# Sigmoid attention and a two-layer network on one core: the products of attention are moved to float32 in the four quarters of the TensorE array

## The chip, the core and the metric

The kernel runs on one core of one Trainium2 chip. The metric is the device time of one launch in microseconds (us); lower is better. "Granted clock" is the share of TensorE's full speed (2.4 GHz) that the profile reports.

## The reference

```python
q, k, v: [8, 12, 448, 64]                      # batch, heads, positions, head size
scores = np.matmul(q, k.transpose(0, 1, 3, 2)) / 8 - np.log(448)
attn = 1.0 / (1.0 + np.exp(-scores))           # a sigmoid, no sum over a row
x = np.matmul(attn, v)                         # -> [8 * 448, 768], heads side by side
h = x @ w_in                                   # [768, 2048]
g = np.maximum(0.01 * h, h)
out = g @ w_out                                # [2048, 768]
```

All inputs and the output are float32.

## The kernel before

The work has three stages, one after the other on TensorE. **Attention** writes x in blocks of [128 columns, 448 positions]. **Stage f** multiplies x by w_in, **stage a** multiplies g by w_out. Stages f and a use sums and differences of blocks (a fast matrix product, so fewer products), and each float32 operand is split there into a high and a low part of type float32r, a type that takes one pass on the array where float32 takes two instructions; a product is then high x high + high x low + low x high. The sums of blocks and the low parts are made on VectorE (DVE), the high parts and copies on ScalarE (ACT).

Attention goes over 48 pairs of heads (`Pair`), two pairs in a *round*, 24 rounds of five *slots*. Program order is kept on every engine: `slot` first emits what is due in the slot by rank (`at`, `later`), then its products; `prepare(room)` then lets VectorE do up to `room` us of other work, which decodes w_in and w_out and builds the sums of their blocks (tiles `wr`, `wd`, `ws`) and the sums of blocks of x (`x_s`). All matrix operations, copies and DMAs are recorded on one helper line, L159, so the trace is read by tile names:

- `qk`: queries and keys of a pair, [2 x 64 rows, 2, 448]: one head in rows 0 to 63, the other in rows 64 to 127. `qks`: their high and low parts.
- `sc_<pair>_<chunk>`: scores in PSUM, [128 keys, 2 heads, 448 queries], for chunks 0 to 2 of 128 keys. A chunk takes 2 heads x 3 products of [64 rows x 128 columns] in float32r: the two heads stand in the upper and lower half of the array.
- `s_<pair>_<chunk>`: the sigmoid of it in SBUF, by ACT, one instruction a chunk.
- The last 64 keys of two pairs are handled together as chunk 3 (`last_scores`): four float32 products of 64 x 64, one in each quarter of the array.
- `pv_<pair>`: the sums with v in PSUM, for both pairs of a round in two banks. A chunk of a pair is two float32 products of [128 rows x 64 columns], one head in each half of the columns (`attn_v`); `last_v` adds chunk 3 with four products in the quarters.
- `x_...`: `Block.keep` copies the two banks to SBUF on ACT, and sums and stores of x follow.

PSUM is used as four buffers of two banks each, for `sc` and `pv` alike. The scores and sums of a round read:

```python
mm(out=ps[:, j, cols], lhsT=self.parts[me, kp, 1, c * P:c * P + P], rhs=self.parts[me, qp, 0, cols], ...)
mm(self.pv[me, :S], lhsT=self.v[:, (NK - 1) * j + c, :], rhs=self.a[c][:, j], start=c == 0, ...)
works = [lambda: whole(x), lambda: whole(y), x.attn_v, y.attn_v, lambda: ending(y, more[0] if more else None)]
```

A float32 product appears in the trace as two instructions of TensorE, a float32r product as one.

Of the kernel before, what the change touches and what calls it, by code (L numbers as in the profile page):

```python
# [12 lines left out]
F32R = mybir.dt.float32r  # L13
# [5 lines left out]
P = 128  # L19


ROOM = 1.7, 2.2, 2.1, 0.7, 0.2
SLOT, READ, STEP, LATE = 2.4, 1.09, 0.7, 1.1
CAST, SOON, HOLD = 3, 2, 4
PAUSE = 1
IDLE = 7


TILES, MORE, LAST, JOIN = 13, 3, 6, 6
RESULTS = 8  # L30
ROTS = 3
EARLY, FIRST, SOON2, JOINT = 12, 9, (2, 5), 26
# [89 lines left out]
def attn_ffn_kernel(ctx: ExitStack, tc: tile.TileContext, qk, v, w_in, w_out, out):  # L122
# [13 lines left out]
    S = qk.shape[3]  # L136
    NP = qk.shape[0] // B
    D = P // 2
    NK = 4
# [9 lines left out]
    heads = [slice(j * D, j * D + D) for j in range(2)]  # L149
# [7 lines left out]
    def pinned(issue):  # L157

        return lambda *args, **kw: tc.keep_in_program_order(issue(*args, **kw))  # L159
# [12 lines left out]
    mm, dma = pinned(nc.tensor.matmul), pinned(nc.sync.dma_start)  # L172
    copy, act, dma_act = (pinned(x) for x in (nc.scalar.copy, nc.scalar.activation, nc.scalar.dma_start))
    vcopy = pinned(nc.vector.tensor_copy)
# [3 lines left out]
    def sub(to, x, y):  # L178
        vec(out=to, in0=x, in1=y, op=ALU.subtract)

    def add(to, x, y):
        vec(out=to, in0=x, in1=y, op=ALU.add)
# [10 lines left out]
    def at(when, rank, *fns):  # L193

        chores.setdefault(when, []).extend((rank, fn) for fn in fns)

    def later(slots, *fns, first=False):
        at(now + slots, 0 if first else 5, *fns)

    def slot(work=None, behind=()):  # L200
        nonlocal now
        todo = sorted(chores.pop(now, ()), key=lambda x: x[0])
        for rank, fn in todo:
            if rank not in behind:
                fn()
        if work is not None:
            work()
        for rank, fn in todo:
            if rank in behind:
                fn()  # L210
        now += 1
# [5 lines left out]
    class Wide:  # L217
# [18 lines left out]
        def high(self):  # L236
            copy(out=self.t[:, 0], in_=self.t[:, 1].bitcast(F32))

        def low(self):
            sub(self.t[:, 1], self.t[:, 1].bitcast(F32), self.t[:, 0])  # L240
# [43 lines left out]
    ps = ExitStack()  # L284
# [37 lines left out]
    def drop(t, slots=1):  # L322
# [3 lines left out]
    attn = ExitStack()  # L326
    vs = attn.enter_context(tc.tile_pool(name="vs", bufs=4, reuse_waits="tile"))
    shift(attn, "pad1", 64)
    raws, spl, ats, made1, wr3 = (attn.enter_context(tc.tile_pool(name=name, bufs=bufs, reuse_waits="tile")) for name, bufs in (
        ("raws", 4), ("spl", 2), ("at", 6), ("sums", 1), ("wr3", 1)))  # L330
    warm = shift(ctx, "warm", 32, "right")
    tiles(ctx, "r", "right", TILES)
    shift(ctx, "pad2", 64, "right")
# [161 lines left out]
    xs, sums = {}, []  # L495

    HALVES = slice(0, S // 2), slice(S // 2, S)
    KEYS = slice(0, 2 * P), slice(2 * P, S)

    SPLIT = slice(0, 2 * S - D)  # L500

    def flat(x):
        return x.rearrange("p a s -> p (a s)")[:, SPLIT]

    class Pair:


# [21 lines left out]
            self.room = t[:, 2 * NK * D:2 * NK * D + 2 * S].rearrange("p (a b) -> p a b", a=2)  # L529
            dma(out=self.v[:, :n], in_=v[self.i, :, :n])  # L530

        def high(self, how=None):
            self.parts = spl.tile([P, 2, 2, S], F32R, tag="qks", name=f"qks_{self.i}")
            (how or copy)(out=flat(self.parts[:, 0]), in_=flat(self.raw))

        def low(self):
            sub(flat(self.parts[:, 1]), flat(self.raw), flat(self.parts[:, 0]))

        def split(self):

            self.parts = spl.tile([P, 2, 2, S], F32R, tag="qks", name=f"qks_{self.i}")
            high, low = self.parts[:, 0], self.parts[:, 1]
            for cols in HALVES:
                copy(out=high[:, 0, cols], in_=self.raw[:, 0, cols])
            for n, cols in enumerate((KEYS[0], slice(2 * P, S - D))):
                vcopy(out=high[:, 1, cols], in_=self.raw[:, 1, cols])
                sub(low[:, 1, cols], self.raw[:, 1, cols], high[:, 1, cols])
                if n == 0:
                    for x in HALVES:
                        sub(low[:, 0, x], self.raw[:, 0, x], high[:, 0, x])  # L550

        def scores(self, h):
            todo, acts = [], []
            for c in range(2 * h, min(2 * h + 2, NK - 1)):
                ps = psum("s", f"sc_{self.i}_{c}")

                for cols in HALVES if self.i == h == 0 else (slice(0, S),):
                    for m, (kp, qp) in enumerate(((0, 0), (0, 1), (1, 0))):
                        for j, me in enumerate(heads):
                            todo.append((c, (m > 0 and c + 1, m, cols.start), dict(  # L560
                                out=ps[:, j, cols], lhsT=self.parts[me, kp, 1, c * P:c * P + P],
                                rhs=self.parts[me, qp, 0, cols], start=m == 0 and cols.start == 0,
                                stop=m == 2 and cols.stop == S, skip_group_check=True)))
                acts.append((c, ps))
            if self.i == h == 0:
                todo.sort(key=lambda x: x[1])
            for n, (c, ps) in enumerate(acts):
                for x in todo if self.i == h == 0 and n == 0 else [x for x in todo if x[0] == c and (self.i or h)]:
                    mm(**x[2])
                self.a.append(self.attn(c, ps))  # L570

        def attn(self, c, ps, s=None):
            if s is None:
# [9 lines left out]
                    mm(ps[rows, j, :S], lhsT=y.raw[me, 1, S - D:], rhs=y.raw[me, 0], start=True, stop=True, skip_group_check=True)  # L583
            self.last = self.attn(NK - 1, ps, pairs[self.i + 1].room)

        def attn_v(self):
            mate = pairs[self.i - 1]
            if self.part == 1:
                self.both = psum("s", f"pv_{self.i}")
            self.pv = (self if self.part == 1 else mate).both[:, self.part - 1]  # L590
            for c in range(NK - 1):
                for j, me in enumerate(heads):
                    mm(self.pv[me, :S], lhsT=self.v[:, (NK - 1) * j + c, :], rhs=self.a[c][:, j], start=c == 0, stop=False,
                       skip_group_check=True)

        def last_v(self):

            x = pairs[self.i - 1]
            for j, me in enumerate(heads):
                for y, rows in ((x, heads[0]), (self, heads[1])):  # L600
                    mm(y.pv[me, :S], lhsT=self.v[rows, 2 * NK - 2 + j, :], rhs=x.last[rows, j],
                       start=False, stop=True, skip_group_check=True)
            block = Block(self.i // 2)
            later(1, lambda: block.keep(x.both), first=True)
            at(now + 2, 8, block.start)

    class Block:
# [7 lines left out]
        def keep(self, pv):  # L615
            xs[self.name] = grab(f"x_{self.p}_{self.name}", F32)
            copy(out=xs[self.name], in_=pv[:, :, :S])

        def store(self, n, t, *gone):

# [56 lines left out]
    pairs = [Pair(i) for i in range(B * NP)]  # L677
# [6 lines left out]
    pairs[1].load_qk()  # L684
    pairs[0].load_v()
    act(out=warm, in_=warm, func=AF.Sigmoid)
    pairs[0].split()
    pairs[2].load_qk()
    pairs[1].load_v()
    next(preps)  # L690
    pairs[1].high(vcopy)
    pairs[1].low()
    pairs[3].load_qk()
    psum = banks("ps_a", dict(s=(4, 2)))

    def whole(x):
        x.scores(0)
        x.scores(1)

    def ending(x, y):  # L700

        if y is not None:
            y.last_scores()
        x.last_v()

    unread = psum("s", "unread")[:, 0]
    for _ in range(IDLE):
        mm(unread[heads[0], :S // 4], lhsT=zeros[:, :D], rhs=zeros, start=True, stop=True)
    slot(lambda: pairs[0].scores(0))
    slot(lambda: pairs[0].scores(1))  # L710
    slot(pairs[0].last_scores)
    rounds = (last + 1) // 2
    items1 = [(p, i, jj) for p in range(NQ) for i in range(len(PRODUCTS1)) for jj in range(2)]
# [6 lines left out]
    for p in range(NQ):  # L720
        for i, n in enumerate(XS):
            if n in XS[:i]:
                continue
            x, t = Own(p, n), when(p, i)
# [5 lines left out]

    for r in range(rounds):
        x, y, *more = pairs[2 * r:2 * r + 6]
        works = [lambda: whole(x), lambda: whole(y), x.attn_v, y.attn_v, lambda: ending(y, more[0] if more else None)]
        if r == 0:

            works = [works[2], works[1], lambda: None, *works[3:]]
        if more:
            z, w = more[:2]
            later(0, z.load_v)
            later(1, w.load_v)  # L740
            later(2, z.high)
            later(3, z.low, w.high)
            later(4, w.low)
        for n, far in enumerate(more[2:]):
            later(1 + 3 * n, far.load_qk)
        for n, work in enumerate(works):
            slot(work)
            prepare(ROOM[n] * (r > 0))

# [17 lines left out]
    psum = banks("ps_f", {f"acc{n}": (1, 2) for n in range(4)})  # L767
# [6 lines left out]
    for g in range(SPLIT1, len(GROUPS1)):  # L774
        for j in range(KQ):
            x = w1[g, j] = Wide(g, j, wb, "wb")
            prepared_by(base + (g - SPLIT1) * 8 + j, x, 0)
    ws = {}
    for p in range(NQ):
        for n, load in STREAM.items():  # L780
            x = ws[p, n] = Streamed(p, n)
# [171 lines left out]
    for q in range(2):  # L953
        for h in range(2):
# [7 lines left out]
            live, last, first = {}, {}, {}  # L962
# [10 lines left out]
            for name, (how, a, b) in sums2[q].items():  # L973
                s = put[q, h, name]
                v = live[name, events[name][0][2]]
                a, b = live[a, name], live[b, name]
# [7 lines left out]
            for i, x in enumerate(PRODUCTS2):  # L984
                k = 2 * NH * q + 2 * i + h
                v = live[x[0], k]
                me = operands[k] = Operand(k, v)
# [194 lines left out]
```

## Time and profile before

| what | value |
|---|---|
| median of 3 runs | 1013.63 us (1013.28 to 1013.64) |
| the profiled execution | 1013.27 us, of which the span from first to last instruction is 1011.5 us |
| attention, until stage f begins | 249.4 us |
| stage f | 384.4 us |
| stage a and the end | 377.7 us |
| TensorE busy | 1006.9 us |

The profile lists busy time by engine, groups of instructions by tile names with the mean duration of one, the idle time before them and what ended it, and the chain of work that ended last. Matmuls are pipelined: a group's mean duration is longer than the distance from one to the next, so distances are read from starts.

### The profile page before, as it was taken

To read this page: it belongs to the slowest core of one execution; us is meant where nothing else is said; L and a number is where in the kernel's file an instruction comes from. 1 tells how busy PE (TensorE), PEld (TensorE's weight loads), DVE (VectorE), ACT (ScalarE), POOL (GpSimd) and SP (SyncE) were. 2 spreads that over 40 slices of the span, in tenths; PEclk is the share of its full clock that TensorE was granted. 3 is DMA by queue.
4 is the path that set the end of the run, shared out by engine and by line. 5 is a ranking of instruction groups with operands and counts; after the bars stand their busy time and mean duration, and the time that the engine had idled before them with its cause. 6 is when DMAs were issued, how large, how long until landed. Compare 5 with 4: busy or idle time off the path is not lost.

```text
span 1011.5 us, 15201 instructions
## 1 busy us (share of the span) xinstructions
PE 1006.9 (100%) x5642; PEld 844.5 (83%) x5642; DVE 853.2 (84%) x1116; ACT 586.2 (58%) x710; POOL 0.3 (0%) x5
## 2 busy tenths in 40 slices
PE   9999999999999999999999999999999999999998
PEld 5555455555999999999999999999999999999998
DVE  5888888887898779888867778799998999999886
ACT  7888888887644454445453655575453456635431
POOL 0000000000000000000000000000000000000000
PEclk9999999999999999999999999999999999999999
DMA  9799899998988997799789979967738698775643
GB/s 326 269 337 370 298 379 324 361 336 276 382 302 241 348 321 266 246 384 311 246 268 315 322 238 362 409 222 255 269 118 321 250 361 326 241 279 164 215 171 109
DMA packets 142025, 291.79 MB, mean 288 GB/s; under 512 B 11136, under 2 KB 71680, under 8 KB 141952
## 3 DMA queue, kind: packets, MB, share of 16 engines
q1 hardware_dynamic: 141088, 290.02, 81.9%
q8 instruction: 44, 0.72, 0.3%
q10 hardware_dynamic: 864, 0.80, 0.2%
q14 instruction: 29, 0.24, 0.1%
HBM read 189.33 MB, written 101.45 MB: 287 GB/s over the span
## 4 chain that ended last, share of the span: by engine, by line
PE 99%; DMA 0%; DVE 0%; ACT 0%; DVEq 0%; issue 0%
PE f L159 38%; PE a L159 36%; PE pv L159 13%; PE sc L159 11%; PE e_z L159 0%; DMA qk<-in_qk 0%; PE e_a L159 0%; DVE o L159 0%; ACT qks L159 0%; DVEq L1178 0%
## 5 line engine op out<-in xcount | busy, mean ns | idle before, releaser
L159 PE MATMUL a<-gh,w 128*128 128x448 f32 x1224 | 342.9, 361 | 0.0
L159 PE MATMUL f<-xh,w 128*128 128x448 f32 x960 | 270.9, 361 | 0.0
L159 PEld LDWEIGHTS a<-gh,w 128*128 128x128 f32 x1224 | 229.3, 187 | 16.9
L159 PE MATMUL a<-gl,w 128*128 128x448 f32 x540 | 196.0, 363 | 0.0
L159 PEld LDWEIGHTS f<-xh,w 128*128 128x128 f32 x960 | 179.9, 187 | 14.3 <-issue 0.7
L159 PE MATMUL f<-xl,w 128*128 128x448 f32 x480 | 174.2, 363 | 0.0
L159 ACT CAST gh<-g 128x896 fp32r<-128x896 f32 x80 | 75.4, 942 | 123.3 <-DVE g L159 108.7
L159 DVE TENSOR_TENSOR h<-h,f 128x896 f32<-128x896 f32 x88 | 95.5, 1085 | 50.4 <-PE f L159 50.2
L159 ACT ACTIVATE s<-sc 128x896 f32<-128x896 f32 x144 | 119.8, 956 | 3.1 <-PE sc L159 3.1
L159 PE MATMUL pv<-s,v 128*64 128x448 f32 x576 | 113.8, 543 | 0.0
L159 ACT COPY h<-f 128x896 f32<-128x896 f32 x56 | 50.1, 910 | 96.5 <-PE f L159 75.2
L159 PEld LDWEIGHTS a<-gl,w 128*128 128x128 f32 x540 | 101.3, 188 | 5.4
L159 DVE TENSOR_TENSOR w<-w 128x768 fp32r<-128x768 f32 x112 | 104.5, 953 | 1.0 <-ACT w L159 1.0
L159 PEld LDWEIGHTS sc<-qks 64*128 64x128 f32 x876 | 79.9, 186 | 23.2 <-issue 16.9
L159 ACT CAST w<-w 128x768 fp32r<-128x768 f32 x112 | 93.1, 832 | 4.0 <-DMA w<-t 4.0
L159 PE MATMUL sc<-qks 64*128 64x448 f32 (+1 forms) x876 | 94.8, 367 | 0.2 <-ACT qks L159 0.2
L159 PEld LDWEIGHTS f<-xl,w 128*128 128x128 f32 x480 | 90.1, 188 | 4.6
L159 PEld LDWEIGHTS pv<-s,v 128*64 128x64 f32 x576 | 39.1, 137 | 63.2 <-issue 54.3
L159 PE MATMUL f<-xh,ws 128*128 128x448 f32 x320 | 91.5, 361 | 0.0
L159 DVE TENSOR_TENSOR gl<-g,gh 128x896 fp32r<-128x896 f32 x72 | 78.3, 1088 | 5.0 <-ACT gh L159 4.5
L159 ACT CAST xh<-xl 128x896 fp32r<-128x896 f32 x64 | 60.3, 944 | 35.5 <-DMA xl<-xd 22.2
L159 DVE TENSOR_TENSOR qks<-qk,qks 128x832 fp32r<-128x832 f32 (+3 forms) x51 | 49.2, 972 | 37.1 <-ACT qks L159 33.9
(79 smaller groups left out, 1072.8 us busy)
## 6 DMA issues: line engine op xcount, KB each, us to landing
w<-t SPq DMA_DIRECT2D x112, 384.0 KB, 4.7
g<-g SPq DMA_DIRECT2D x81, 448.0 KB, 5.8
xl<-xd SPq DMA_DIRECT2D x64, 448.0 KB, 6.4
g<-h SPq DMA_DIRECT2D x64, 448.0 KB, 6.0
qk<-in_qk SPq DMA_DIRECT2D x46, 448.0 KB, 5.6
xd<-x_s SPq DMA_DIRECT2D x36, 448.0 KB, 6.8
xd<-x SPq DMA_DIRECT2D x28, 448.0 KB, 6.6
wr<-in_w_in SPq DMA_DIRECT2D x24, 512.0 KB, 6.6
```

The source lines that it names most:

```text
L159: return lambda *args, **kw: tc.keep_in_program_order(issue(*args, **kw))
```

## The change

- Queries and keys are no longer split: `high`, `low` and `split` go, with the ACT casts and the VectorE subtractions that made `qks`, and its pool. The pool of `qk` has six buffers where it had four.
- A chunk of scores is four float32 products of [64 rows x 64 columns], one in each quarter: head j in rows, each half of the chunk's 128 keys in columns.
- The sums with v take both pairs at once. A chunk's 128 keys are two halves of 64 rows, so a product is [64 rows x 64 columns] and there are two accumulators, `pv_<pair>_0` and `pv_<pair>_1`: into the first goes the upper half of the first pair and the lower half of the second, into the second the other two halves. Chunk 3 goes into the first.
- `Block.keep` copies the second accumulator with ACT a slot earlier than before; a new `Block.add` adds the first one on VectorE, where the copy was before. PSUM still has four buffers of two banks.
- The first slots: all chunks of pair 0 in one slot, no wait for a split. One warm-up product fewer (`IDLE` 6). The shares of `prepare` (`ROOM`) are spread evenly with the same total, 6.9. One tile of x more for the whole run and one fewer later (`TILES`, `MORE`).

```diff
-ROOM = 1.7, 2.2, 2.1, 0.7, 0.2
+ROOM = 1.4, 1.4, 1.4, 1.4, 1.3
...
-TILES, MORE, LAST, JOIN = 13, 3, 6, 6
+TILES, MORE, LAST, JOIN = 14, 2, 6, 6
...
+        def scores(self, c):
+            ps = psum("s", f"sc_{self.i}_{c}")
+            for j, me in enumerate(heads):
+                for n, rows in enumerate(heads):
+                    keys = slice(c * P + n * D, c * P + n * D + D)
+                    mm(ps[rows, j, :S], lhsT=self.raw[me, 1, keys], rhs=self.raw[me, 0], start=True, stop=True,
+                       skip_group_check=True)
+            self.a.append(self.attn(c, ps))
...
+        def attn_v(self, c):
+
+            x = pairs[self.i - 1]
+            if c == 0:
+                self.both = []
+            for n in range(2):
+                if c == 0:
+                    self.both.append(psum("s", f"pv_{x.i}_{n}"))
                 for j, me in enumerate(heads):
-                    mm(self.pv[me, :S], lhsT=self.v[:, (NK - 1) * j + c, :], rhs=self.a[c][:, j], start=c == 0, stop=False,
-                       skip_group_check=True)
+                    for m, (y, rows) in enumerate(((x, heads[n]), (self, heads[1 - n]))):
+                        mm(self.both[n][me, m, :S], lhsT=y.v[rows, (NK - 1) * j + c, :], rhs=y.a[c][rows, j],
+                           start=c == 0, stop=n == 1 and c == NK - 2, skip_group_check=True)
+            if c == NK - 2:
+                self.block = Block(self.i // 2)
+                later(1, lambda: self.block.keep(self.both[1]), first=True)
...
-            block = Block(self.i // 2)
-            later(1, lambda: block.keep(x.both), first=True)
+            block = self.block
+            later(1, lambda: block.add(self.both[0]), first=True)
             at(now + 2, 8, block.start)
...
+        def add(self, pv):
+            add(xs[self.name], xs[self.name], pv[:, :, :S])
...
+        works = [
+            several((x.scores, 0), (y.scores, 0), (x.scores, 1)), several((y.scores, 1), (x.scores, 2), (y.scores, 2)),
+            several((y.attn_v, 0)), several((y.attn_v, 1), (y.attn_v, 2)), lambda: ending(y, more[0] if more else None)]
...
-            later(2, z.high)
-            later(3, z.low, w.high)
-            later(4, w.low)
```

TensorE, the scores of one whole round and the sums with v that follow, before; each `x6` is one chunk, and the output's 128 rows are all columns of the array:

```order
L159 MATMUL sc_4_0_495<-qks_4_451 128x448 x6
L159 MATMUL sc_4_1_496<-qks_4_451 128x448 x6
L159 MATMUL sc_4_2_513<-qks_4_451 128x448 x6
L159 MATMUL sc_5_0_528<-qks_5_464 128x448 x6
L159 MATMUL sc_5_1_529<-qks_5_464 128x448 x6
L159 MATMUL sc_5_2_546<-qks_5_464 128x448 x6
L159 MATMUL pv_4_563<-s_4_0_503,v_4_381 64x448 x2
L159 MATMUL pv_4_563<-s_4_1_511,v_4_381 64x448 x2
L159 MATMUL pv_4_563<-s_4_2_520,v_4_381 64x448 x2
L159 MATMUL pv_4_563<-s_5_0_536,v_5_415 64x448 x2
L159 MATMUL pv_4_563<-s_5_1_544,v_5_415 64x448 x2
L159 MATMUL pv_4_563<-s_5_2_553,v_5_415 64x448 x2
```

The same place in a round of the changed kernel, to the end of the first chunk's sums:

```order
L159 MATMUL sc_6_0_571<-qk_6_378 64x448 x4
L159 MATMUL sc_7_0_578<-qk_7_437 64x448 x4
L159 MATMUL sc_6_1_585<-qk_6_378 64x448 x4
L159 MATMUL sc_7_1_604<-qk_7_437 64x448 x4
L159 MATMUL sc_6_2_611<-qk_6_378 64x448 x4
L159 MATMUL sc_7_2_618<-qk_7_437 64x448 x4
L159 MATMUL pv_6_0_627<-s_6_0_576,v_6_455 64x448
L159 MATMUL pv_6_0_627<-s_7_0_583,v_7_482 64x448
L159 MATMUL pv_6_0_627<-s_6_0_576,v_6_455 64x448
L159 MATMUL pv_6_0_627<-s_7_0_583,v_7_482 64x448
L159 MATMUL pv_6_1_632<-s_6_0_576,v_6_455 64x448
L159 MATMUL pv_6_1_632<-s_7_0_583,v_7_482 64x448
```

The chunks of the two pairs alternate now, each is four products of 64 x 64 in place of six, and a chunk's sums are eight products of 64 x 64, four for each accumulator, where a pair's chunk took two of 128 rows.

VectorE near the end of a round before; `qks` rows are the low parts of the next round's queries and keys, the others are work of `prepare`:

```order
L159 TENSOR_TENSOR ws0_0_557<-wd0_0_410,ws0_0_557 128x2x128
L159 TENSOR_TENSOR qks_6_561<-qk_6_417,qks_6_561 128x832
L159 TENSOR_TENSOR ws0_0_557<-ws0_0_557,wd0_0_410 128x2x128
L159 TENSOR_SCALAR wd0_1_591<-wr0_1_0_466 128x512
L159 TENSOR_TENSOR qks_7_577<-qk_7_476,qks_7_577 128x832
L159 TENSOR_SCALAR wd0_1_591<-wd0_1_591 128x512 x2
L159 SCALAR_TENSOR_TENSOR wd0_1_591<-wr0_1_0_466,wd0_1_591 128x512
L159 TENSOR_TENSOR x_0_s8_677<-x_0_10_379,x_0_20_607 128x896
```

The same place in the changed kernel:

```order
L159 TENSOR_TENSOR ws0_0_519<-ws0_0_519,wd0_0_372 128x2x128
L159 TENSOR_SCALAR wd0_1_566<-wr0_1_0_439 128x512
L159 TENSOR_TENSOR x_0_20_544<-x_0_20_544,pv_4_0_509 128x896
L159 TENSOR_SCALAR wd0_1_566<-wd0_1_566 128x512 x2
L159 SCALAR_TENSOR_TENSOR wd0_1_566<-wr0_1_0_439,wd0_1_566 128x512
L159 TENSOR_TENSOR x_0_s8_625<-x_0_10_334,x_0_20_544 128x896
L159 TENSOR_TENSOR x_0_s13_637<-x_0_s5_507,x_0_20_544 128x896
L159 SCALAR_TENSOR_TENSOR wd0_1_566<-wr0_1_0_439,wd0_1_566 128x512
```

The two `qks` rows are gone, and the row `x_0_20_544<-x_0_20_544,pv_4_0_509` has come in: it reads the first accumulator, so it waits for the last product of its round, and all of `prepare` that follows on VectorE waits behind it.

## Rows read from the trace of the kernel before

**Rows 1.** The page: span; busy us of each engine (share, instructions).

```profile
span 1011.5 us, 15201 instructions
PE 1006.9 (100%) x5642; PEld 844.5 (83%) x5642; DVE 853.2 (84%) x1116; ACT 586.2 (58%) x710; POOL 0.3 (0%) x5
```

**Rows 2.** Windows by stage: busy by engine (instructions), clock, DMA share, GB/s.

```profile
0.00:16.30 16.30, 15.05 (x112) 8.77 (x112) 5.55 (x12) 10.38 (x14) 0.31 (x5) 1.00 0.89 325
16.30:249.40 233.10, 233.10 (x1741) 125.04 (x1741) 196.43 (x340) 197.02 (x262) 0.00 (x0) 1.00 0.93 328
249.40:633.80 384.40, 384.40 (x1921) 360.09 (x1922) 309.25 (x430) 195.94 (x221) 0.00 (x0) 1.00 0.89 304
```

**Rows 3.** The chain that ended last, in order of time: start, us, what.

```profile
3.70 0.39 ACT qks L159
4.08 0.04 issue
4.13 3.64 PE sc L159 x33
...
16.29 3.84 PE sc L159 x36
...
26.46 3.84 PE sc L159 x36
30.30 4.66 PE pv L159 x24
34.96 0.91 PE sc L159 x8
35.88 0.75 PE pv L159 x8
36.63 3.84 PE sc L159 x36
...
249.38 384.39 PE f L159 x1920
```

**Rows 4.** Timeline of the weight loads (PEld) inside one round.

```profile
25.16 0.15 PEld L159 LDWEIGHTS pv<-v 64*64 64x64 f32 x4 [0.22 <-issue]
25.53 0.15 PEld L159 LDWEIGHTS pv<-v 64*64 64x64 f32 x4 [0.22 <-issue]
...
30.66 0.14 PEld L159 LDWEIGHTS pv<-s,v 128*64 128x64 f32 x2 [0.23 <-issue]
...
34.04 0.14 PEld L159 LDWEIGHTS pv<-s,v 128*64 128x64 f32 x2 [0.23 <-issue]
```

**Rows 5.** Timeline, all engines, of the same round and its end.

```profile
27.38 4.99 ACT L159 ACTIVATE s<-sc 128x896 f32<-128x896 f32 x6
...
35.70 0.93 PE L159 MATMUL pv<-v 64*64 64x448 f32 x8
...
35.94 0.92 ACT L159 ACTIVATE v<-sc 128x896 f32<-128x896 f32 x1 [2.04 <-PE sc L159]
```

**Rows 6.** Groups of DVE and ACT, 16.3 to 249.3: busy, mean ns, idle.

```profile
L159 DVE TENSOR_TENSOR qks<-qk,qks 128x832 fp32r<-128x832 f32 x45 | 45.9, 1023 | 30.5 <-ACT qks L159 27.4 <-DMA xd<-x_s 1.7 <-DMA ts<-ws 1.3
...
L159 ACT CAST qks<-qk 128x832 fp32r<-128x832 f32 x44 | 38.1, 953 | 0.0
L159 ACT COPY x<-pv 128x896 f32<-128x896 f32 x23 | 20.8, 904 | 0.0
```

**Rows 7.** The page's groups: VectorE adding from PSUM.

```profile
L159 DVE TENSOR_TENSOR h<-h,f 128x896 f32<-128x896 f32 x88 | 95.5, 1085 | 50.4 <-PE f L159 50.2
```

**Rows 8.** Timeline of the first microseconds, ACT's queue and TensorE's warm-up.

```profile
0.73 1.38 ACTq L159 DMA_DIRECT2D qk<-in_qk  x3
1.03 2.88 PE L159 MATMUL unread<-zeros 128*64 128x112 f32 x14 [1.03 <-DVE zeros L682]
5.98 0.33 SPq L159 DMA_DIRECT2D qk<-in_qk  x1
```

**Rows 9.** DMA issues at 1.1:1.6 and 5.9:6.3: KB each, us to landing.

```profile
qk<-in_qk ACTq DMA_DIRECT2D x2, 112.0 KB, 3.0
...
qk<-in_qk SPq DMA_DIRECT2D x1, 448.0 KB, 7.7
```

**Rows 10.** Waits from 249 to 256: who waited for whom, us, times, longest.

```profile
ACT x L159 <- DMA xd<-x_s: 3.4, 1, 3.4
...
PEld f L159 <- ACT x L159: 0.3, 1, 0.3
```

More of the change, by code (lines that the diff above doesn't have):

```diff
@@ L25 @@
 PAUSE = 1
-IDLE = 7
-TILES, MORE, LAST, JOIN = 13, 3, 6, 6
+IDLE = 6
+TILES, MORE, LAST, JOIN = 14, 2, 6, 6
 RESULTS = 8
@@ L328, in attn_ffn_kernel @@
     shift(attn, "pad1", 64)
-    raws, spl, ats, made1, wr3 = (attn.enter_context(tc.tile_pool(name=name, bufs=bufs, reuse_waits="tile")) for name, bufs in (
-        ("raws", 4), ("spl", 2), ("at", 6), ("sums", 1), ("wr3", 1)))
+    raws, ats, made1, wr3 = (attn.enter_context(tc.tile_pool(name=name, bufs=bufs, reuse_waits="tile")) for name, bufs in (
+        ("raws", 6), ("at", 6), ("sums", 1), ("wr3", 1)))
     warm = shift(ctx, "warm", 32, "right")
@@ L498, in attn_ffn_kernel @@
     KEYS = slice(0, 2 * P), slice(2 * P, S)
-    SPLIT = slice(0, 2 * S - D)
-    def flat(x):
-        return x.rearrange("p a s -> p (a s)")[:, SPLIT]
     class Pair:
@@ L530, in load_v @@
             dma(out=self.v[:, :n], in_=v[self.i, :, :n])
[L532 to L570, printed above, removed]
+        def scores(self, c):
[6 more added lines that the diff above has]
+            self.a.append(self.attn(c, ps))
@@ L584, in last_scores @@
             self.last = self.attn(NK - 1, ps, pairs[self.i + 1].room)
[L586 to L591, printed above, removed]
-                for j, me in enumerate(heads):
-                    mm(self.pv[me, :S], lhsT=self.v[:, (NK - 1) * j + c, :], rhs=self.a[c][:, j], start=c == 0, stop=False,
-                       skip_group_check=True)
+        def attn_v(self, c):
[5 more added lines that the diff above has]
+                    self.both.append(psum("s", f"pv_{x.i}_{n}"))
+                for j, me in enumerate(heads):
+                    for m, (y, rows) in enumerate(((x, heads[n]), (self, heads[1 - n]))):
[4 more added lines that the diff above has]
+                later(1, lambda: self.block.keep(self.both[1]), first=True)
         def last_v(self):
@@ L599, in last_v @@
             for j, me in enumerate(heads):
-                for y, rows in ((x, heads[0]), (self, heads[1])):
-                    mm(y.pv[me, :S], lhsT=self.v[rows, 2 * NK - 2 + j, :], rhs=x.last[rows, j],
+                for m, (y, rows) in enumerate(((x, heads[0]), (self, heads[1]))):
+                    mm(self.both[0][me, m, :S], lhsT=self.v[rows, 2 * NK - 2 + j, :], rhs=x.last[rows, j],
                        start=False, stop=True, skip_group_check=True)
-            block = Block(self.i // 2)
-            later(1, lambda: block.keep(x.both), first=True)
+            block = self.block
+            later(1, lambda: block.add(self.both[0]), first=True)
             at(now + 2, 8, block.start)
@@ L686, in attn_ffn_kernel @@
     act(out=warm, in_=warm, func=AF.Sigmoid)
-    pairs[0].split()
     pairs[2].load_qk()
@@ L690, in attn_ffn_kernel, with several @@
     next(preps)
-    pairs[1].high(vcopy)
-    pairs[1].low()
     pairs[3].load_qk()
     psum = banks("ps_a", dict(s=(4, 2)))
-    def whole(x):
-        x.scores(0)
-        x.scores(1)
+    def several(*fns):
+        return lambda: [fn(c) for fn, c in fns]
     def ending(x, y):
@@ L708, in attn_ffn_kernel @@
         mm(unread[heads[0], :S // 4], lhsT=zeros[:, :D], rhs=zeros, start=True, stop=True)
-    slot(lambda: pairs[0].scores(0))
-    slot(lambda: pairs[0].scores(1))
+    slot(several(*((pairs[0].scores, c) for c in range(NK - 1))))
     slot(pairs[0].last_scores)
@@ L732, in attn_ffn_kernel @@
         x, y, *more = pairs[2 * r:2 * r + 6]
-        works = [lambda: whole(x), lambda: whole(y), x.attn_v, y.attn_v, lambda: ending(y, more[0] if more else None)]
+        works = [
+            several((x.scores, 0), (y.scores, 0), (x.scores, 1)), several((y.scores, 1), (x.scores, 2), (y.scores, 2)),
+            several((y.attn_v, 0)), several((y.attn_v, 1), (y.attn_v, 2)), lambda: ending(y, more[0] if more else None)]
         if r == 0:
-            works = [works[2], works[1], lambda: None, *works[3:]]
+            works[:2] = several((y.scores, 0)), several((y.scores, 1), (y.scores, 2))
         if more:
```

## The prediction

> **What bounds the kernel now.** I read the page's busy times first: TensorE is busy 1006.9 of 1011.5 us [rows 1]. The windows by stage then show that this holds in each stage: from 16.3 to 249.4 us it is busy the whole time, VectorE 196.4 and ScalarE 197.0 of 233.1 us, and the DMA engines 93% [rows 2]. The chain of work that ended last shows why nothing else counts: apart from the first 4 us it is TensorE alone, and one round of attention is the same four pieces each time, 3.84 us of scores, 4.66 of sums with v, 0.91 and 0.75 of chunk 3, in all 10.17 us (26.46 to 36.63) [rows 3]. So a change in attention is worth what it does to these pieces. What it takes from VectorE and ScalarE is worth nothing by itself, and a wait that it adds costs only where TensorE comes to stand.
>
> **The unit.** The timeline of weight loads gives the pace of float32 products. In the sums with v, loads come in twos, one for each half of the columns, the first at 30.66 and the last at 34.04 with nine distances between: 0.376 us each. In chunk 3 they come in fours, one for each quarter, at 25.16 and 25.53: 0.37 us [rows 4]. So a step of 0.376 us carries two half-array or four quarter-array instructions. A float32 product is two instructions, so a group of four products in the quarters takes two steps, 0.752 us.
>
> In these steps the round before is 12 steps of sums (4.51 us), 4 of chunk 3 (1.50), and 36 float32r instructions, two at a time, for the scores (3.84). The pieces of the chain for sums and chunk 3 are 0.15 and 0.16 us longer than their steps [rows 3]; there the array changes between halves of columns, quarters and halves of rows.
>
> **The scores (added work).** Six chunks of six float32r products become six groups of four float32 products: 6 x 0.752 = 4.51 us in place of 3.84. This is the loss: +0.67 a round.
>
> **The sums and chunk 3.** Six chunks of two products become six groups of four: 12 steps, 4.51 us, as many as before. Chunk 3 keeps its four steps. What goes is the change of shape, 0.15 and 0.16 us, since the whole round stands in the quarters. The round is then 28 steps x 0.376 = 10.53 us against 10.17: **+0.36 us**. Bounds of the step, from the quarters' own two starts, which are given to 0.01: 0.37 (10.36 a round, +0.19) and 0.38 (10.64, +0.47), which is 4 us less and 2.6 more in 24 rounds. I take 0.376, the distance over nine steps.
>
> **The whole of attention.** Scores of the second round begin at 16.29 us and stage f at 249.38: 233.09 us [rows 3]. After: 22 whole rounds (22 x 10.53 = 231.6), a last one without chunk 3's scores (26 steps, 9.8) and about 0.1 for the change to the full array: 241.5, or **+8.4 us**.
>
> **The start.** The split goes: 0.39 us on ScalarE stood between the load and the first product at 4.13 [rows 3]. But the first scores now need all queries of pair 0. Their second half is the second of three issues on ACT's queue in 1.38 us from 0.73, so at about 1.2, and lands 3.0 us later, at 4.2 [rows 8, 9]. So nothing is won there. From 4.2 there are 30 steps to the second round (three groups, chunk 3, three groups, six of sums, chunk 3 and its sums): 11.3 us, which ends at 15.5. The warm-up instructions show 0.206 us each for 112 columns (2.88 over 14) [rows 8], where 0.376 for 448 would be 0.094, so the array is at half pace at first; one group at half pace adds up to 0.75. I take half of that: 15.9, or **-0.4**, within -0.8 and 0. The keys of pair 3, issued at 5.98 and landed 7.7 us later at 13.7, are wanted at about 14.4, so they are in time [rows 8, 9].
>
> **Stage f.** On ScalarE its instructions are the same in the same order, and VectorE has five operations of `prepare` less. One stall goes: the copy of the last block waited 3.4 us for a store and held TensorE's loads for 0.3 us [rows 10]; its place in PSUM is no longer the one that the second group wants: **-0.3**, or 0 if another wait takes its place.
>
> **The waits that come in.** (1) VectorE's add of the first accumulator. It can start some 0.24 us after chunk 3's sums give up the array, as the sigmoid did at 35.94 after 35.70 [rows 5], and takes 1.09, the duration of an add from PSUM [rows 7]: done 1.33 us into the next round. It frees the buffer of the fourth group of scores, which starts at 2.26 and whose weights may load one step earlier, so 0.55 to 0.93 us are spare. Behind the add on VectorE stands `prepare` and behind that the weights' casts on ScalarE. VectorE's own load falls from 196.4/22.9 = 8.57 us a round to 7.6 (two subtractions of 1.02 less [rows 6], one add more) of 10.53, so on average it should already be waiting when the products end. (2) ScalarE's copy of the second accumulator, one slot earlier; it frees the second group's buffer and has chunk 3's sigmoid behind it. ScalarE gives out six sigmoids in 4.99 us, so one in about 0.81 [rows 5], where a group takes 0.752: the sixth is done 6.0 us into the round and is wanted at 7.5, the first is done at 1.95 and its buffer is wanted at 3.0. The copy starts at 9.3, ends at 10.2, and is wanted at 11.3. ScalarE has two casts of 0.95 less [rows 6]. All spare times are above 0.5 us, so I put the waits at 0, with a bound of 0.5 us a round, +11.5 in all.
>
> **The sum.** 1013.27 (the profiled execution; its span is 1.8 shorter, which stays) + 8.4 - 0.4 - 0.3 = 1021.0. The median of the runs shown is 0.36 higher, so I forecast **1021.3 us**, +0.8%. A measurement of this kernel can tell about 0.2%, 2 us, from no change.
>
> **Rivals.**
> *VectorE comes late to the add.* For it: VectorE has waited in attention up to 1.7 us for a store and 1.3 for another [rows 6], at operations of the kind that now stand ahead of the add. Against it: 30.5 us of its idle time were spent waiting for ScalarE's casts, which go [rows 6]. From 0.55 us late on, TensorE stands for what is beyond. Half a microsecond in every round is 1033; 1 us in a third of them 1029.
> *The quarters don't hold their pace over a long stream.* Four per step has been seen for only four steps on end. The scores issue 36 products and 36 loads in 3.84 us, 0.053 each [rows 3]; if that were the limit of issue, eight in a step would take 0.427, a round 11.95 and the kernel 1013.3 + 24 x 1.78 = 1056. Against it: chunk 3 shows 0.37 with eight [rows 4].
> The Trainium skill, "TensorE: Matmul & The Clock Gate", section "Measured speedup vs the span model", reports 3.07 for four tiles by rows, not 4; by that, an estimate, a step would be 0.49 us, a round 13.7 and the kernel about 1098. The loads at 25.16 and 25.53 speak against it.
> *Stages f and a get faster.* Their products take 384.39/1920 = 0.200 us [rows 3], and 448 columns take 0.188 in half a float32 step. If the difference were traffic of VectorE and ScalarE, and the shifted work of VectorE eased it, 2.1 ns less on each of some 3,790 products would cancel the loss and 5 ns give 1002. Against it: these stages' instructions are the same but for five.
> For attention itself to be no slower, a step would have to fall under 10.17/28 = 0.363, which no row shows.
>
> **How the numbers follow.** My forecast, 1018 to 1024 with the start's and the step's bounds: 0.70. VectorE late: 0.16, mostly below 1030. Pace lost: 0.06. Stages f and a faster: 0.05 beyond 2 us, 0.03 within. So slower 0.92, same 0.03, faster 0.05. The range of 8 in 10 is 1018.5 to 1030: the forecast but for a step of just 0.37, and most of the late add.
>
> **What would show it.** A round of 28 steps with starts 0.376 apart and no piece longer; attention to about 257 us; stages f and a at 384 and 378 as before; the add's wait ended by TensorE, not TensorE's by the add. I am wrong if TensorE shows idle time ahead of the fourth group of scores, if quarter steps are longer than 0.38 in a long run, or if stage f changes.

## The result, and the profile after

| | before | after |
|---|---|---|
| median | 1013.4 us (6 runs, 1013.03 to 1013.64) | 1022.56 us (6 runs, 1021.38 to 1023.57) |
| profiled execution; its span | 1013.27; 1011.5 us | 1022.32; 1020.5 us |

The ratio is 1.009, with a 95% interval of 1.0077 to 1.0103: the changed kernel is slower by 0.9%, where 1021.3 us was forecast.

The page's first rows after the change, which answer to [rows 1], and the windows of its start and of attention, which answer to [rows 2]:

```profile
span 1020.5 us, 16673 instructions
PE 1015.5 (100%) x6492; PEld 820.3 (80%) x6492; DVE 830.7 (81%) x1086; ACT 552.1 (54%) x662; POOL 0.3 (0%) x5
```

```profile
0.00:16.00 16.00, 14.28 (x120) 7.20 (x124) 0.15 (x1) 7.46 (x10) 0.30 (x5) 1.00 0.88 319
16.00:257.00 241.00, 241.00 (x2572) 101.46 (x2568) 177.99 (x319) 165.03 (x217) 0.00 (x0) 1.00 0.91 317
```

The clock of 1.00 in the first row needs care: the trace holds no clock record before 7.51 us, and the windows count time without a record as full speed (see the last section).

VectorE and ScalarE have less to do, 178.0 and 165.0 us of 241 where they had some 196 and 197 of 233. TensorE is still busy the whole time, so that relief is worth nothing. Its own work has grown, and the chain of work (start, us, what) shows where; it answers to [rows 3].

```profile
4.22 7.10 PE sc L159 x56
...
17.33 4.51 PE sc L159 x48
...
27.86 4.51 PE sc L159 x48
32.37 4.51 PE pv L159 x48
36.88 0.75 PE sc L159 x8
37.63 0.75 PE pv L159 x8
38.38 4.51 PE sc L159 x48
...
258.62 384.21 PE f L159 x1920
```

A round runs from 27.86 to 38.38 us: 4.51 + 4.51 + 0.75 + 0.75 = 10.52, against 10.17. From the second round to stage f it is 258.62 - 17.33 = 241.29 us against 233.09: +8.20. The start costs 17.33 - 16.29 = +1.04 more, and stage f 0.18 less. Together +9.06, and the profiled execution is 9.05 longer.

TensorE waits for no buffer. All waits of TensorE in the whole execution are its warm-up and the first load; in attention the add on VectorE waits for TensorE, not the other way round:

```profile
PE unread L159 <- DVE zeros L655: 1.0, 1, 1.0
PE sc L159 <- DMA qk<-in_qk: 0.7, 1, 0.7
...
DVE x L159 <- PE pv L159: 70.4, 22, 16.5
```

The timeline of the weight loads shows the pace, in the first microseconds and inside a round (first and last of 17 groups on end); it answers to [rows 4].

```profile
4.99 0.28 PEld L159 LDWEIGHTS sc<-qk 64*64 64x64 f32 x4 [0.47 <-issue]
5.74 0.28 PEld L159 LDWEIGHTS sc<-qk 64*64 64x64 f32 x4 [0.47 <-issue]
...
7.23 0.28 PEld L159 LDWEIGHTS sc<-qk 64*64 64x64 f32 x4 [0.47 <-issue]
7.75 0.16 PEld L159 LDWEIGHTS sc<-qk 64*64 64x64 f32 x4 [0.24 <-PE sc L159]
...
59.24 0.16 PEld L159 LDWEIGHTS sc<-qk 64*64 64x64 f32 x4 [0.22 <-issue]
...
65.26 0.16 PEld L159 LDWEIGHTS pv<-s,v 64*64 64x64 f32 x4 [0.22 <-issue]
```

From 59.24 to 65.26 are 16 steps, 0.376 us each, across the border from scores to sums. At the start the steps are twice as long, 0.75 us, until 7.23; the next, from 7.23 to 7.75, is the last long one. So two things are to be told apart by experiments: what makes the round longer (theory: steps and changes of shape alone; rival: something that waits, such as the add), and what makes the start longer.

### The profile page after: what moved, and what is told of

The parts are those of the page before. It is cut to its first block, busy times and chain, and to the rows that moved or that the text cites. A ratio compares the mean times of both kernels' runs of the same rounds, so it can differ in the third digit from the quotient of the medians.

```text
span 1020.5 us, 16673 instructions
## 1 busy us (share of the span) xinstructions
PE 1015.5 (100%) x6492; PEld 820.3 (80%) x6492; DVE 830.7 (81%) x1086; ACT 552.1 (54%) x662; POOL 0.3 (0%) x5
## 4 chain that ended last, share of the span: by engine, by line
PE 99%; DMA 0%; ACTq 0%; DVE 0%; DVEq 0%; issue 0%
PE f L159 38%; PE a L159 36%; PE sc L159 13%; PE pv L159 12%; PE e_z L159 0%; DMA qk<-in_qk 0%; PE e_a L159 0%; ACTq L159 0%; DVE o L159 0%; DVEq L1144 0%
## 5 line engine op out<-in xcount | busy, mean ns | idle before, releaser
L159 PE MATMUL sc<-qk 64*64 64x448 f32 x1344 | 136.7, 542 | 0.7 <-DMA qk<-in_qk 0.7
L159 PEld LDWEIGHTS sc<-qk 64*64 64x64 f32 x1344 | 53.6, 135 | 74.7 <-issue 65.2
L159 PE MATMUL pv<-s,v 64*64 64x448 f32 x1152 | 112.7, 536 | 0.0
L159 PEld LDWEIGHTS pv<-s,v 64*64 64x64 f32 x1152 | 45.7, 133 | 62.6 <-issue 60.7
L159 DVE TENSOR_TENSOR x<-x,pv 128x896 f32<-128x896 f32 x24 | 26.1, 1088 | 70.4 <-PE pv L159 70.4
L159 DVE TENSOR_TENSOR xl<-xl,xh 128x896 fp32r<-128x896 f32 x64 | 69.5, 1085 | 13.0 <-ACT xh L159 13.0
```

## The experiments

**The scores alone.** The scores are those of the changed kernel, the sums those of before.

```diff
-            several((y.attn_v, 0)), several((y.attn_v, 1), (y.attn_v, 2)), lambda: ending(y, more[0] if more else None)]
+            x.attn_v, y.attn_v, lambda: ending(y, more[0] if more else None)]
...
+                    mm(self.pv[me, :S], lhsT=self.v[:, (NK - 1) * j + c, :], rhs=self.a[c][:, j], start=c == 0, stop=False,
...
+            later(1, lambda: block.keep(x.both), first=True)
```

> One half of the change alone: the scores are float32 products in the quarters as in the changed kernel, the products with v are those of before (128 rows, one pair after the other), ScalarE copies both sums and VectorE adds none. Theory (a round is the sum of its steps of 0.376 us and of about 0.1 to 0.2 us at each change of tile shape, and nothing waits): 4.51 + 4.66 + 0.91 + 0.75 = 10.8 us a round against 10.17 before and 10.53 after, so 1027 to 1029 us: this half costs more than the whole change. Rival (scores in quarters cost no more than the split ones, and the whole rise comes from the sums and their add on VectorE): 10.2 us a round, 1013 to 1016 us.

Measured: 1030.54 us, 1.0159 times before (1.0144 to 1.0174), a little above the range expected. The chain of one round:

```profile
28.90 4.51 PE sc L159 x48
33.41 4.66 PE pv L159 x24
38.07 0.91 PE sc L159 x8
38.98 0.75 PE pv L159 x8
39.74 4.51 PE sc L159 x48
```

The round is 10.84 us, as the theory has it, with 4.66 and 0.91 just as in [rows 3]. This half of the change costs 0.67 us a round where the whole costs 0.35: the sums in quarters give back 0.32. The excess over the expected range lies ahead of the second round, which begins at 18.07 us in this kernel, 1.78 later than before; without these 1.78 us the time would be 1028.8, inside the range.

**The price of a change of shape.** One tiny product on all 128 rows, read by nobody, stands behind chunk 3's scores in the changed kernel.

```diff
+            mm(ps[heads[0], 0, S:S + 16], lhsT=self.raw[:, 1, S - D:], rhs=self.raw[:, 0, :16], start=True, stop=True)
```

> The changed kernel with one tiny product more in each round (all 128 rows, 64 columns of the array, 16 columns of queries, a result that nobody reads) behind the last scores: it is over in a few hundredths of a us, but TensorE changes the tile shape there and back. Theory (a change of shape costs 0.1 to 0.2 us, which is where the change got back 0.31 us of a round): 0.25 to 0.4 us more a round, 10.78 to 10.93 us, 1028 to 1032 us. Rival (a change of shape costs nothing, and what looked like it was something else, such as the order of the products): no more than 0.05 us a round, 1022 to 1024 us.

Measured: 1032.61 us, 1.0183 (1.0169 to 1.0196). Its chain:

```profile
4.16 8.71 PE sc L159 x58
...
104.60 0.97 PE sc L159 x10
105.57 0.91 PE pv L159 x8
...
115.50 0.97 PE sc L159 x10
```

The round is 10.90 us (104.60 to 115.50), 0.38 more than in the changed kernel, and it sits in the two pieces around the tiny product: 0.97 and 0.91 where 0.75 and 0.75 were. So going to another tile shape and back costs 0.3 to 0.4 us, and the 0.32 us that the sums gave back are of that size. The time is again a little above the expected range through what lies ahead of the second round, which begins at 19.26 us in its chain (the first 58 instructions took 8.71 us).

**The cover of the add.** The add is done twice over.

```diff
-            add(xs[self.name], xs[self.name], pv[:, :, :S])
+            t = xs[self.name]
+            sub(t, t, pv[:, :, :S])
+            vec_st(out=t, in0=pv[:, :, :S], scalar=2.0, in1=t, op0=ALU.mult, op1=ALU.add)
```

> The changed kernel with the add of the sums done twice over on VectorE (a subtraction, then twice the sum added to it: the same result, two instructions of about 1.09 and 1.2 us instead of one of 1.09). Theory: the add has 0.55 to 0.93 us of cover in a round before TensorE wants its buffer, so an add that is 1.1 to 1.2 us longer shows a wait of 0.2 to 0.6 us in each of 23 rounds: 1027 to 1036 us, and the wait names VectorE's second instruction. Rival A (the add lies on the path already): all of 1.15 us a round, 1049 us. Rival B (far more cover than that): no wait, 1022 to 1023 us.

Measured: 1033.16 us, 1.0187 (1.0172 to 1.0201). The chain of one round, which now turns to VectorE once:

```profile
31.35 2.49 PE sc L159 x24
...
39.98 1.10 DVE x L159
...
41.10 1.10 DVE x L159
...
42.34 2.49 PE sc L159 x24
```

From 31.35 to 42.34 the round is 10.99 us, 0.47 more, for an add that ends 1.12 us later (41.10 - 39.98). So some 0.65 us were spare, inside the 0.55 to 0.93 of the prediction: the single add costs nothing, and of the 1.12 us that a second one brings 0.47 are paid.

**The start.** First the pause between warm-up and first scores is filled with three more warm-up products (`IDLE` 6 to 9).

```diff
-IDLE = 6
+IDLE = 9
```

> The changed kernel with nine warm-up products instead of six, so that TensorE is busy until the first queries and keys have landed. In the changed kernel it paused 0.69 us there, and its first 36 score instructions took 5.22 us where the later ones take 0.094 us each (3.4 us). Theory: the pause is what puts the first products at half pace. Then the second round begins at 15.5 to 15.9 us instead of 17.33, and the time falls by 1.4 to 1.8 us to about 1021, with a smaller spread between runs. Rival: the slow beginning has another cause (the landing of the columns that each product reads); then the pause goes but the second round still begins at about 17.3 us, and the time stays at 1022.5.

Measured: 1021.63 us (1021.0 to 1023.48), 1.0074 (1.0060 to 1.0087), which the interval does not part from the changed kernel. The weight loads at its start:

```profile
4.58 0.31 PEld L159 LDWEIGHTS sc<-qk 64*64 64x64 f32 x8 [0.28 <-issue]
5.39 0.25 PEld L159 LDWEIGHTS sc<-qk 64*64 64x64 f32 x4 [0.50 <-issue]
6.13 0.21 PEld L159 LDWEIGHTS sc<-qk 64*64 64x64 f32 x4 [0.50 <-issue]
6.58 0.14 PEld L159 LDWEIGHTS sc<-qk 64*64 64x64 f32 x4 [0.23 <-issue]
```

There is no pause, and the first steps still take 0.74 to 0.81 us; they grow short 1.2 us earlier, but the scores also begin 0.4 us later. The second round begins at 17.00 instead of 17.33 in the chain. My theory that the pause makes the slow pace fell: the slow pace is there without one.

Then the warm-up products are made wider, and eight of them instead of six: 128 rows by 112 columns of the array, by the profile, where they were 128 by 64 (the expectation's "112 rows" is a slip).

```diff
-IDLE = 6
+IDLE = 8
...
-        mm(unread[heads[0], :S // 4], lhsT=zeros[:, :D], rhs=zeros, start=True, stop=True)
+        mm(unread[:S // 4, :S // 4], lhsT=zeros, rhs=zeros, start=True, stop=True)
```

> The changed kernel with eight warm-up products that fill 112 rows and 112 columns of the array, in place of six on 112 rows and 64 columns... that is, longer and wider, ending about when the first queries and keys have landed (4.2 us). Theory: what the array does in the first microseconds decides when its full pace comes, and wide products bring it at about 5.2 us, as in the kernel before, where the warm-up was followed by wide products (half pace lasted until about 7.7 us in the changed kernel and 6.4 us with nine narrow warm-up products). Then the second round begins at 15.8 to 16.3 us instead of 17.33, and the time is 1020.5 to 1021.5 us. Rival: it is the same 6.4 us or later whatever the warm-up's width: second round at 16.9 or later, 1021.5 to 1022.5 us.

Measured: 1022.08 us (1021.09 to 1023.03), 1.0079 (1.0066 to 1.0091). The weight loads:

```profile
4.29 0.23 PEld L159 LDWEIGHTS sc<-qk 64*64 64x64 f32 x8 [0.20 <-issue]
4.75 0.14 PEld L159 LDWEIGHTS sc<-qk 64*64 64x64 f32 x4 [0.23 <-issue]
...
7.96 0.24 PEld L159 LDWEIGHTS sc<-qk 64*64 64x64 f32 x8 [1.20 <-DMA qk<-in_qk]
```

Now the steps are short from the first scores on. But TensorE then comes to the second pair's queries and keys before they have landed, and its next loads stand until 7.96. After six steps of 0.376 us from 4.29 it would have gone on at 6.55; the chain has it at 8.00:

```profile
1.66 6.20 DMA qk<-in_qk
8.00 2.86 PE sc L159 x27
...
17.24 4.13 PE sc L159 x44
```

What the pace gave, the transfer took: 1.45 us. The chain dates a first instruction of the second round at 16.86 and the bulk of it at 17.24, where the changed kernel has 17.33, and stage f begins at 258.52 us instead of 258.62. So only 0.10 us are won. Without the wait the second round would begin at about 15.8 (17.24 - 1.45, an estimate); 15.9 was the forecast. The measured time lies where the expectation's rival put it, but for another reason than the rival's. In this execution the transfer took 6.2 us, in the changed kernel's 5.0, so how long the wait is differs between executions. Whether it was the width that brought the short steps so early, one execution can't show; the last section comes back to it.

**The sums alone.** Queries and keys are split and scored as before; the products with v stay in quarters, and copy and add both follow the last of them.

```diff
-                later(1, lambda: self.block.keep(self.both[1]), first=True)
...
-            later(1, lambda: block.add(self.both[0]), first=True)
+            later(1, lambda: block.keep(self.both[1]), lambda: block.add(self.both[0]), first=True)
...
+            later(2, z.high)
+            later(3, z.low, w.high)
+            later(4, w.low)
```

> The other half alone: queries and keys are split and scored as before, but chunk by chunk for the two pairs in turn; the products with v are float32 in quarters for two pairs at once, the copy of one sum on ScalarE and the add of the other on VectorE following the last of them. Theory of steps: 3.84 + 4.51 + 0.75 + 0.75 = 9.85 us and a change of shape or two, 9.9 to 10.05 us a round, 1007 to 1011 us, faster than both kernels, if no buffer waits. Rival: the copy (0.91 us) and then the add (1.09 us) free the buffers of the sums some 0.5 us later than the scores of the next round want them, or VectorE, with the subtractions of the split and the add both, falls behind; then the chain of work shows waits for VectorE in each round, 10.4 us a round or more, 1018 us or more.

Measured: 1025.81 us, 1.0114 (1.0098 to 1.0130): the rival was right. TensorE's timeline, with the waits in brackets, and its waits in all:

```profile
37.07 2.10 PE L159 MATMUL sc<-qks 64*128 64x448 f32 x18
39.35 2.08 PE L159 MATMUL sc<-qks 64*128 64x448 f32 x18 [0.18 <-DVE x L159]
```

```profile
PE sc L159 <- DVE x L159: 5.2, 23, 0.6
PE f L159 <- ACT x L159: 2.5, 1, 2.5
```

The add comes too late in every round, and at the end stage f waits 2.5 us for the last copy. After this wait the clock was granted at half for some 3 us (the last section has the rows), and stage f takes 385.88 us where it took 384.39 before. So taken one by one, both halves of the change lose more than the whole. For this half that is no property of the products; it is the place of the copy and the add. The next kernel moves them: the second sum is finished first and copied early, into a part of v's tile that nobody uses.

```diff
+            if n == 1 and c == NK - 2:
+                copy(out=x.room, in_=self.both[1][:, :, :S])
...
+            xs[self.name] = grab(f"x_{self.p}_{self.name}", F32)
+            add(xs[self.name], t, pv[:, :, :S])
...
+            several((y.attn_v, 1, 0), (y.attn_v, 1, 1), *((z.last_scores,) for z in more[:1])),
+            several((y.attn_v, 0, 0), (y.attn_v, 1, 2), (y.attn_v, 0, 1)), several((y.attn_v, 0, 2), (y.last_v,))]
```

> The sums alone once more (split scores, the products with v in quarters for two pairs), mended where the first trial waited: the products of the second sum end earlier in the round, so that ScalarE copies it into a spare part of a tile of v while TensorE still works on the first sum; VectorE's add then follows the last product at once, and the buffer that it frees is wanted as the fourth of the next round's scores, not as the third. Theory (steps and changes of shape, no wait): 3.84 + 6 times 0.75 + 0.75 + 0.75 and 0.1 for a change, 9.95 to 10.05 us a round against 10.17 before, 1007.5 to 1011 us, faster than both kernels. Rival: VectorE has too much to do in 10 us a round (217 us of 241 were busy in the first trial) and comes late to the add or to the split of the next queries and keys whatever the order; then TensorE's waits name VectorE again, 10.3 us a round or more, 1017 us or more.

Measured: 1015.54 us, 1.0018 (1.0009 to 1.0027), between the two. Its undisturbed rounds are as the theory has them, 10.00 us (29.28 to 39.28 in the chain), but its second round began 2.9 us later than before, and VectorE came late in four others, by the waits in all. From the second round to stage f it is 233.00 us against 233.09 before, so the late rounds cost what the others gained. Most of the late start goes with the clock: in this execution the first record of the full clock begins at 10.52 us, before at 5.21, and half of the difference is 2.66 us, an estimate of what that cost.

```profile
19.19 3.91 PE sc L159 x36
...
29.28 3.83 PE sc L159 x36
...
39.28 3.83 PE sc L159 x36
```

```profile
PE sc L159 <- DVE x L159: 1.4, 4, 0.4
```

The mended kernel has the wide warm-up, sets the last scores of the first round back, and casts the next queries and keys earlier. A second version also prepares 0.3 us a round less of the weights (`ROOM` 1.6, 2.1, 2.1, 0.6, 0.2).

```diff
+            works[3:] = several((y.attn_v, 0, 0), (y.attn_v, 1, 2), (y.attn_v, 0, 1)), several((y.attn_v, 0, 2), *ahead, (y.last_v,))
...
-            later(2, z.high)
-            later(3, z.low, w.high)
-            later(4, w.low)
+            later(2, z.high, w.high)
+            later(3, z.low, w.low)
```

> The second trial of the sums alone with three places mended: the wide warm-up, the last scores of the first round set back behind products that have their operands (TensorE waited there for a later pair's queries and keys), and both casts of the next queries and keys on ScalarE ahead of the last scores' sigmoid, so that VectorE gets to the add sooner. The second trial ran its undisturbed rounds in 10.01 us against 10.17 before, but began its second round at 19.1 us against 16.2, and VectorE came late to the add in some six rounds, 0.2 to 0.7 us each. Theory: 22 rounds at 10.01 us and a second round that begins at 16.3 to 17.0 us end attention 2 to 4 us earlier than before: 1010 to 1012.5 us, faster than both kernels. Rival: VectorE, over 90% busy in these rounds, falls behind in other rounds instead; then waits of 2 to 4 us remain and the time is 1013 to 1015 us.

> The same with 0.3 us a round less of the preparation of weights put into attention (its planner's budgets are 6.6 us a round instead of 6.9; the rest is done in the next stage). Theory: VectorE is in time in more rounds: 0 to 1.5 us less than the kernel with the full budgets. Rival: the preparation that is left over comes late in the next stage, and TensorE waits there: 1 us or more on top.

Measured: 1012.02 us, 0.9982 (0.9973 to 0.9991), and 1011.81 us, 0.9977 (0.9968 to 0.9985). Both are faster than both kernels; the two are not told apart by their intervals. The chain of the second:

```profile
17.10 3.83 PE sc L159 x36
...
103.34 0.75 PE sc L159 x8
...
113.36 0.75 PE sc L159 x8
...
247.43 384.36 PE f L159 x1920
```

A round is 10.02 us (103.34 to 113.36). From the second round to stage f it is 230.33 us against 233.09, 2.76 less; the start, 17.10 against 16.29, takes 0.81 of it back. Which of the mends brought VectorE in time was not tried one by one. A control asks whether the wide warm-up alone does it; it is the kernel before with the one line changed that is shown above:

> The kernel before with the wide warm-up alone (seven products on 112 rows and 112 columns instead of 64 columns): how much of the mended kernels' gain is the warm-up's. Theory: the kernel before reached full pace at 5.2 us already, so no more than 0.6 us can be had: 1012.8 to 1013.6 us. Rival: its start is bound by pace as that of the changed kernel is: 1012 us or less.

Measured: 1013.54 us, 0.9997 (0.9987 to 1.0006). It does nothing there: its eleven runs (1013.10 to 1014.08) and those of the mended kernels (up to 1012.77) do not touch. So the wide warm-up alone is not the gain; by the chain the gain lies in the rounds, with the sums.

## Why the prediction was right, and where it was off

**The step.** Predicted 0.376 us for four quarter instructions, measured 0.376 over 16 steps on end. The rival that the quarters lose their pace in a long stream is out. The Trainium skill's figure of 3.07 times for four row tiles ("TensorE: Matmul & The Clock Gate", section "Measured speedup vs the span model") would have made the round 13.7 us, an estimate; the trace does not show that loss in quarters of 64 rows, and the measured 10.52 decides. The page's figure is for tiles of 32 rows, of which no run here tells anything.

**The round.** Predicted 10.53, measured 10.52. The two terms behind it were each tried alone: +0.67 for the scores (10.84 against 10.17) and -0.32 for the shape (10.52 against 10.84), where +0.67 and -0.31 were predicted; the tiny product shows that such a change has a price. The scores alone lose 0.67 and the sums alone gain 0.17 (10.00), which makes +0.50 and not +0.35. The 0.15 between them is about one change of shape: the one between scores and sums goes only if both are in quarters. This was worked out, not tried.

**Attention.** Predicted 241.5 us from the second round on, measured 241.29.

**The waits.** Predicted 0, measured 0; the doubled add puts the spare time at some 0.65 us. VectorE's lateness, the rival with the highest chance, does not occur in this kernel. It does occur where copy and add both follow the last product, as the sums alone showed (23 waits, 5.2 us). With the copy moved ahead and the split's subtractions kept, four waits were left (1.4 us), and in the second version of the mended kernel none for the add.

**Stage f.** Predicted -0.3, measured -0.18 (384.21 against 384.39). The wait of 0.3 us of TensorE's loads for the copy is gone, as predicted.

**The start: the term that was mis-sized.** Predicted -0.4 within -0.8 and 0, measured +1.04, outside the bounds. The step of the prediction that failed is "one group at half pace adds up to 0.75. I take half of that". It took the slow pace for something that ends with the first group. In fact there are five such steps between 4.22 and 7.75, 3.53 us instead of 1.88: 1.65 lost instead of 0.38. That is 1.27 of the 1.44 us between forecast and measurement. With it the second round begins at 4.22 + 30 x 0.376 + 1.65 = 17.15 us, which is where TensorE's timeline has it; the chain dates the same piece 0.18 later:

```profile
17.15 3.19 PE L159 MATMUL sc<-qk 64*64 64x448 f32 x32
```

The trace's clock records date the end of the slow pace: the full clock is recorded from 7.51 us on, and half of 7.51 - 4.22 is these 1.65 us. In the kernel before it is recorded from 5.21 on, and half of 5.21 - 4.13 is 0.54. The difference of 1.11 is as large as the whole +1.04 of the start. Executions that begin with the same instructions on TensorE differ in this moment by 2.0 to 5.9 us (the last section has them), half of which is as much or more, so the +1.04 is not shown to be the change's doing.

The bound was wrong for another reason too: once the pace is right, the second pair's landing can set the start, as the wide warm-up showed (8.00 us instead of 6.55), and no term looked at it. The forecast as a whole held because 1.4 us is small beside 8, not because the start was understood.

## What to carry to other kernels

Where one engine is busy throughout, find the step in which its instructions go, count steps and changes of tile shape, and leave out what other engines save. A change of two halves may hide a good one: here the float32 scores lose 0.67 us a round and the joint sums can gain 0.17, but only after the copy and the add had been moved to where nobody waits for them. The first microseconds need a sum of their own, with every pair's landing time in it, not only the first's, and with the time at half clock, which differs between executions.

## What the runs showed of the hardware

**The first products run at half pace until the first record of the full clock.** The windows give a granted clock of 1.00 from 0 to 16 us in the changed kernel, and yet its steps take twice the time until 7.2 us. The trace's own list of clock records tells why: its first record, with the share 1.00 (2.4 GHz), begins at 7.51 us, and before it there is none. In every trace the steps grow short where this first record begins, and where it begins ahead of the first scores they are short from the start. No record names the level ahead of it; twice the step is what the lower level, 1.2 GHz, gives (the sums alone show it below). These are the moments, in us from the start of the span:

| warm-up products, then the first scores | first record of the full clock begins |
|---|---|
| six, 128 by 64; quarters | changed kernel 7.51, scores alone 8.31, add twice over 8.60, tiny product 9.93 |
| nine, 128 by 64; quarters | no pause 6.27 |
| eight, 128 by 112; quarters | wide warm-up 4.40 |
| seven, 128 by 64; split | before 5.21, sums alone 4.58, with early copy 10.52 |
| seven, 128 by 112; split | before with wide warm-up 3.86, mended 4.15, its second version 6.17 |

A pause is not needed for the half pace: nine products without one had it too. But executions that begin with the same instructions on TensorE lie far apart (4.58 and 10.52; 7.51 to 9.93; 4.15 and 6.17). The four with wide products come early and the eight with narrow ones mostly later, with an overlap, and each kernel has one trace. So it is not shown that the width or the number of the warm-up products sets the moment. Half of the differences within the first row is 1.2 us, which could be part of the 2.2 us over which the changed kernel's runs spread, where those of before beside them spread over 0.6; this stays open, and beside the experiments the kernel before had single runs of up to 1016.33 us too.

**After a wait of 2.5 us the clock fell.** In the sums alone TensorE stood from 257.47 to 259.99 us, ahead of stage f. The windows of that trace give a clock of 0.50 (1.2 GHz) from 261 to 264 us and of 1.00 from 264 to 268. The products of stage f start 0.37 us apart in the first stretch and 0.20 in the second. Stage f took 1.49 us longer than before (385.88 against 384.39), on top of the wait itself.

**The idle time shown for a wait is about half of what the wait costs here.** With the doubled add the round grew by 0.47 us, where the wait shown for it is 0.24:

```profile
PE sc L159 <- DVE x L159: 5.5, 23, 0.2
```

```profile
39.64 2.46 PE L159 MATMUL sc<-qk 64*64 64x448 f32 x24
42.34 2.49 PE L159 MATMUL sc<-qk 64*64 64x448 f32 x24 [0.24 <-DVE x L159]
```

It is 5.5 us in 23 waits. The first three groups of scores are six steps, 2.26 us, so the fourth would begin at 41.90; it begins at 42.34, 0.44 later. The idle time counts only from 42.10, the end that is shown for the group before (39.64 + 2.46), which lies 0.20 behind its last step. So what a wait costs is read from starts.
